# One whole K or V tile in every 50 MB of traffic is sent over four DMA engines

## The chip, the cores and the metric

The kernel runs on one core of one Trainium2 chip. The core has a matrix engine (TensorE, called PE in the profile), a vector engine (DVE), a scalar engine (ACT), a general engine (POOL), a queue engine (SP) that issues most transfers here, and sixteen DMA engines that move the data between the chip's memory (HBM) and the on-chip memory (SBUF, 128 partitions). The metric is the device time of one execution in microseconds (us): the median of several runs. Lower is better.

## The reference

Two layers run twice, in the order A, B, A, B, and the gradient of everything with respect to the input, both caches and all weights is returned with the output. Layer A is one decode step of grouped-query attention over a long cache; layer B is a two-layer MLP on one token for each of two batch rows.

```python
B, Sq, D = 2, 1, 1024
Hq, Hkv, Sk, Dh = 32, 4, 16384, 128        # A: 32 query heads share 4 cached K/V heads, 16384 positions
F = 3584                                    # B: hidden width

def _A_ref(x, k_cache, v_cache, wq, wo):
    q = heads(x @ wq)
    k = jnp.repeat(k_cache, 8, axis=1); v = jnp.repeat(v_cache, 8, axis=1)
    p = _softmax(jnp.einsum("bhqd,bhkd->bhqk", q, k) * (Dh ** -0.5))
    o = jnp.einsum("bhqk,bhkd->bhqd", p, v)
    return merge(o) @ wo
def _B_ref(x, w1, b1, w2, b2):
    return _gelu(_layernorm(x) @ w1 + b1) @ w2 + b2
# x -> x + A(ln x) -> x + B(ln x) -> x + A(ln x) -> x + B(ln x); then jax.vjp with grad_out
```
(`heads` and `merge` stand for reshapes that are cut here.) Everything is bfloat16. K and V are 33.5 MB each, and the gradients of K and V are as large again. Since the work for each cached value is small, the kernel is largely a matter of moving bytes: K and V are read for both forward passes, for the first backward pass and once more for the second one, and the two cache gradients are written.

## The kernel before: how tiles are loaded and stored

The cache is cut into tiles of 1 MB: 128 partitions, each with 32 positions of 128 values, so one run of 8192 bytes for each partition. Seven such buffers (`ld`) are filled in turn by SP; eight more tiles (and two extra) stay resident between the passes.

```python
    LDW = 4096
    NLD = 7
    ld = ctx.enter_context(tc.tile_pool(name="ld", bufs=NLD))
    ... # cut
    def w_load(W, j0, rb, n_cols):
        wt = ld.tile([128, LDW], BF16, name="wt", tag="ld")
        wv = wt[:, 0:rb * n_cols].rearrange("p (j n) -> p j n", j=rb)
        nc.sync.dma_start(wv, W[j0 * 128:(j0 + rb) * 128, :].rearrange("(j p) n -> p j n", p=128))
        return wv
    ... # cut
    Kv = A_k_cache.rearrange("b h (p t) d -> (b h) p t d", p=128)
    Vv = A_v_cache.rearrange("b h (p t) d -> (b h) p t d", p=128)
    ... # cut
    def kv_load(w, g, c):
        keep = w + str(c) if g == G - 1 else w if (g, c) == (XG, 0) else None
        t = held_tiles[keep] if keep else ld.tile([128, LDW], BF16, name="kv_" + w, tag="ld")
        if keep not in held:
            src = Kv if w == "K" else Vv
            nc.sync.dma_start(t[:].rearrange("p (t d) -> p t d", d=128), src[g, :, c * TC:(c + 1) * TC, :])
            if keep:
                held.add(keep)
        return t[:].rearrange("p (t d) -> p t d", d=128)
```

A forward pass (`attn_fwd`) walks over slots of eight 128x128 blocks: TensorE turns a block of K (the name `tp`), DVE or ACT copies it out (`kT`), TensorE makes the scores (`sc`); blocks of V go straight into the weighted sum (`acc_all`). The first backward pass (`attn_bwd`) does the like with both. The second one is the last stage of the kernel. It loads K, V and slices of wq through a list of jobs into whatever tile is free, and it writes the gradients of the caches and the weights:

```python
    def store(out_ap, view, tile_):
        pace["queue"].dma_start(out_ap, view)        # POOL's queue; SP's for the last few
        if tile_ is not None:
            by_store.append(tile_)
    ... # cut
    def load_next():
        job = jobs.popleft()
        t = loaded[job] = load_tile()                # may have to wait for a store to land
        open_loads.append(job)
        if job[0] == "wq":
            src = wq_v[:, job[2]:job[2] + 4, job[1] * D:(job[1] + 1) * D]
            nc.sync.dma_start(t[:].rearrange("p (j n) -> p j n", j=4), src)
        else:
            src = (Kv if job[0] == "K" else Vv)[job[1], :, job[2] * TC:(job[2] + 1) * TC, :]
            nc.sync.dma_start(t[:].rearrange("p (t d) -> p t d", d=128), src)

    def pump(most, spare):
        while jobs and len(open_loads) < most and n_free() > spare:
            load_next()
```

Of the kernel before, what the change touches and what calls it, by code (L numbers as in the profile page):

```python
# [2 lines left out]

# [20 lines left out]
def kernel(  # L24
# [24 lines left out]
    nc = tc.nc  # L49
# [4 lines left out]
    B, _, D = A_x.shape  # L54
# [11 lines left out]
    TC = 32  # L66
# [23 lines left out]
    ps_x = ctx.enter_context(tc.tile_pool(name="ps_x", bufs=4, space=PSUM))  # L90
    ps_acc = ctx.enter_context(tc.tile_pool(name="ps_acc", bufs=1, space=PSUM))
    ps_sm = ctx.enter_context(tc.tile_pool(name="ps_sm", bufs=1, space=PSUM))

    def pt(shape, dtype, name):
        return ps_tp.tile(shape, dtype, name=name, tag="tp")
# [74 lines left out]
    def wide_in(x2):  # L170

        return x2.unsqueeze(1).to_broadcast([128, WIDE // 2, 2])

    def wide_out(ps, c0):

        return ps[:, c0:c0 + WIDE].rearrange("p (a b) -> p a b", b=2)
# [77 lines left out]
    def w_load(W, j0, rb, n_cols):  # L254
        wt = ld.tile([128, LDW], BF16, name="wt", tag="ld")
        wv = wt[:, 0:rb * n_cols].rearrange("p (j n) -> p j n", j=rb)
        nc.sync.dma_start(wv, W[j0 * 128:(j0 + rb) * 128, :].rearrange("(j p) n -> p j n", p=128))
        return wv

    class BwdPipe:  # L260
# [57 lines left out]
    def turn(view, new_tp):  # L318

        tp = new_tp()  # L320
        for o in range(8):
            PE.transpose(tp[:, o, :], view[:, o * 128:(o + 1) * 128], ident[:])  # L322
        evac_bf16(view, tp[:].rearrange("p a b -> p (a b)"), 1024)
# [19 lines left out]
    class Ahead:  # L343
# [9 lines left out]
        def load(self, k):  # L353
            j0, rb = self.chunks[k]
            wv = w_load(self.W, j0, rb, D)
            for j in range(rb):
                self.rows[j0 + j] = wv[:, j, :]
# [46 lines left out]
    def kv_load(w, g, c):  # L404
        keep = w + str(c) if g == G - 1 else w if (g, c) == (XG, 0) else None
        t = held_tiles[keep] if keep else ld.tile([128, LDW], BF16, name="kv_" + w, tag="ld")
        if keep not in held:
            src = Kv if w == "K" else Vv
            nc.sync.dma_start(t[:].rearrange("p (t d) -> p t d", d=128), src[g, :, c * TC:(c + 1) * TC, :])
            if keep:  # L410
                held.add(keep)
        return t[:].rearrange("p (t d) -> p t d", d=128)
# [462 lines left out]
    wq_v = A_wq.rearrange("(j p) n -> p j n", p=128)  # L875

    def wq_steps(l, kv, dqT, dn, new_tp, new_ps, get_=None, done_=lambda *job: None):

        hs = slice(kv * 8, kv * 8 + 8)
        box = {}  # L880

        def load(j):
            wt = ld.tile([128, LDW], BF16, name="wqt", tag="ld") if get_ is None else get_("wq", kv, j)
            box[j] = wt[:].rearrange("p (j n) -> p j n", j=4)
            if get_ is None:
                nc.sync.dma_start(box[j], wq_v[:, j:j + 4, kv * D:(kv + 1) * D])

        def turn_row(j):
            turn(box[j - j % 4][:, j % 4, :], new_tp)

        def products(j0=0):
            ps = new_ps()
            for j in range(j0, DJ):
                for o in range(8):
                    PE.matmul(wide_out(ps, 2 * j), lhsT=box[j - j % 4][:, j % 4, o * 128:(o + 1) * 128],
                              rhs=wide_in(dq_all[:, kv * 8 + o, 2 * l:2 * l + 2]), start=(o == 0), stop=(o == 7))
            V.tensor_tensor(out=dn[:, j0:DJ], in0=dn[:, j0:DJ],
                            in1=ps[:, 2 * j0:2 * DJ].rearrange("p (j b) -> p j b", b=2), op=ALU.add)
            for j in (0, 4):
                done_("wq", kv, j)  # L900

        def dq_in():
            for b in range(2):
                V.tensor_copy(out=dq_all[:, hs, 2 * l + b], in_=dqT[:, b * HKV + kv, :])

        return [lambda j=j: load(j) for j in (0, 4)], dq_in, [lambda j=j: turn_row(j) for j in range(DJ)], products, box
# [31 lines left out]
    for k in range(NLD - 2, len(w2b.chunks)):  # L938
        w2b.load(k)
        j0, rb = w2b.chunks[k]  # L940
# [193 lines left out]
    def load_tile():  # L1134
        return (by_read or by_store if opening["on"] else by_store or by_read).popleft()

    def store(out_ap, view, tile_):
        pace["queue"].dma_start(out_ap, view)
        if tile_ is not None:
            by_store.append(tile_)  # L1140

# [10 lines left out]
    def dbias(rows, i, n, out_ap, name):  # L1152
        p = 32 * i
        row = new_home()
        for c0 in range(0, n, 512):
            ps = mx()
            PE.matmul(ps[p:p + 1, :], lhsT=ones_bf[p:p + 4, 0:1], rhs=rows[p:p + 4, c0:c0 + 512], start=True, stop=True,
                      tile_position=(p, p))
            evac_cast(row[p:p + 1, c0:c0 + 512], ps[p:p + 1, :], 512)
        store(out_ap.rearrange("(o f) -> o f", o=1), row[p:p + 1, 0:n], row)  # L1160

    def dw_units(xrows, yrows, i, chunks, y0, ny, out_of):

        ps_, tpos = (slice(0, 128), None) if i is None else (slice(32 * i, 32 * i + 4), (32 * i, 0))
        box = {}
        units = []
        for j0, rb in chunks:
            for j in range(rb):
                for c0 in range(0, ny, 512):
                    def u(j0=j0, rb=rb, j=j, c0=c0):  # L1170
                        if j == 0 and c0 == 0:
                            box["t"], box["n"] = new_home(), 2 if i is None or pace["short"] else rb
                        sv_ = box["t"][:, 0:rb * ny].rearrange("p (j n) -> p j n", j=rb)
                        ps = mx()
                        PE.matmul(ps[:], lhsT=xrows[ps_, (j0 + j) * 128:(j0 + j + 1) * 128],  # L1175
                                  rhs=yrows[ps_, y0 + c0:y0 + c0 + 512], start=True, stop=True, tile_position=tpos)
                        evac_cast(sv_[:, j, c0:c0 + 512], ps[:], 512)
                        if c0 + 512 >= ny and (j % box["n"] == box["n"] - 1 or j == rb - 1):
                            js = j - j % box["n"]
                            store(out_of(j0 + js, j + 1 - js), sv_[:, js:j + 1], box["t"] if j == rb - 1 else None)  # L1180
                    units.append(Unit(u, j == 0 and c0 == 0))
        return units
# [15 lines left out]
    def load_next():  # L1198
        job = jobs.popleft()
        t = loaded[job] = load_tile()  # L1200
        open_loads.append(job)
        if job[0] == "wq":
            src = wq_v[:, job[2]:job[2] + 4, job[1] * D:(job[1] + 1) * D]
            nc.sync.dma_start(t[:].rearrange("p (j n) -> p j n", j=4), src)
        else:
            src = (Kv if job[0] == "K" else Vv)[job[1], :, job[2] * TC:(job[2] + 1) * TC, :]
            nc.sync.dma_start(t[:].rearrange("p (t d) -> p t d", d=128), src)

    def pump(most, spare):
        while jobs and len(open_loads) < most and n_free() > spare:  # L1210
            load_next()
# [35 lines left out]
    def kv_pair(w, i, h):  # L1247

        g, c = chunks[i]
        if h == 0:  # L1250
            stgs[w, i] = new_home()
        sv_ = stgs[w, i][:].rearrange("p (b r t d) -> p b r t d", r=4, t=2, d=128)
        blk, Qm = blks[w, i], qms[w, g]
        o = 0 if w == "V" else NB
        pss = [mx() for _ in range(4)]
        for b in range(2):
            for r in range(4):
                PE.matmul(pss[r][:, b * 256:(b + 1) * 256], lhsT=blk[32 * r:32 * r + 32, o + 2 * h + b, :],  # L1258
                          rhs=Qm[32 * r:32 * r + 32, :, :].rearrange("p a b -> p (a b)"), start=True, stop=True,
                          tile_position=(32 * r, 0))  # L1260
        for r in range(4):
            evac_cast(sv_[:, 2 * h:2 * h + 2, r], pss[r][:].rearrange("p (b t d) -> p b t d", b=2, t=2), 512)
        if h == 0:
            split[w, i] = pace["short"] or i >= NC - 2
        if h == 1 or split[w, i]:
            lo = h if split[w, i] else 0
            dst = (dVv if w == "V" else dKv)[g, :, c * TC + lo * TC // 2:c * TC + (h + 1) * TC // 2, :]
            store(dst, stgs[w, i][:, lo * LDW // 2:(h + 1) * LDW // 2].rearrange("p (t d) -> p t d", d=128),
                  stgs[w, i] if h == 1 else None)
# [214 lines left out]
    i, g = NC - 1, order[-1]  # L1484
    kv = g % HKV
# [57 lines left out]
```

## Time and profile before

| what | before |
|---|---|
| median of 3 runs | 1142.67 us (1141.52 to 1146.9) |
| span of the profiled run | 1136.9 us |
| TensorE matmul busy | 944.5 us (83%) |
| DVE busy | 633.7 us (56%) |
| ACT busy | 564.7 us (50%) |
| bytes moved by DMA | 449.31 MB, mean 395 GB/s |
| HBM read, written | 348.14 MB, 98.58 MB |

A profile page gives for each engine the busy time, then the span in 40 slices (here 28.4 us each) with the busy tenths of the engines, the share of the sixteen DMA engines that was busy and the rate. The queues of the transfers have numbers: q1 holds what SP issues, q0 what POOL issues, q8 and q14 fetch the engines' own instructions:

```profile
## 3 DMA queue, kind: packets, MB, share of 16 engines
q1 hardware_dynamic: 74448, 354.46, 77.4%
q0 software_dynamic: 17360, 92.29, 19.7%
q8 instruction: 137, 2.24, 0.7%
q14 instruction: 38, 0.31, 0.1%
```

The last column is the time of a queue's packets as a share of what sixteen engines could give in the span. Together these are 97.9%.

The trace also holds, for each transfer, sixteen marks: [...] the transfer counts as landed with the last.

### The profile page before, as it was taken

Reading aid. Unit: us, or ns where it says so; the run is one execution under the profiler, and the core shown is the slowest. Engines: PE = TensorE matmul, PEld = TensorE weight load, DVE = VectorE, ACT = ScalarE, POOL = GpSimd, SP = SyncE. Lnnn points to the kernel's source line nnn. Section 1 sums busy time; section 2 is a strip of 40 time slices with the busy share of each in tenths; the row PEclk is TensorE's granted clock in tenths of the full one; section 3 lists DMA queues with packets and bytes.
Section 4 is the critical chain, followed back from the end, with each engine's and each line's share of the span. In section 5 each row is a group of like instructions: output and inputs, shape, how many; then the busy total and the mean of one; then the engine's idle time right before and its main releaser. Section 6 shows DMA issues by size and latency. Waiting matters only on the chain.

```text
span 1136.9 us, 40053 instructions
## 1 busy us (share of the span) xinstructions
PE 944.5 (83%) x17566; PEld 730.9 (64%) x17567; DVE 633.7 (56%) x1356; ACT 564.7 (50%) x1415; POOL 70.9 (6%) x126
## 2 busy tenths in 40 slices
PE   4989895487879885899988689989898989999884
PEld 3867674487767665888876578855555555555551
DVE  1545451133545432554846454678877868786784
ACT  0535351022535340343554344667777767786673
POOL 0000000000000000000000000022111112111210
PEclk9989796596999876899998799998987868896895
DMA  8999999998999989999999999998999999999996
GB/s 370 424 425 423 425 424 413 409 378 354 424 425 423 425 310 413 408 369 411 367 422 418 351 359 355 346 378 318 376 421 423 421 419 421 421 422 420 423 423 256
DMA packets 91983, 449.31 MB, mean 395 GB/s; under 512 B 7318, under 2 KB 7318, under 8 KB 54688
## 3 DMA queue, kind: packets, MB, share of 16 engines
q1 hardware_dynamic: 74448, 354.46, 77.4%
q0 software_dynamic: 17360, 92.29, 19.7%
q8 instruction: 137, 2.24, 0.7%
q14 instruction: 38, 0.31, 0.1%
HBM read 348.14 MB, written 98.58 MB: 393 GB/s over the span
## 4 chain that ended last, share of the span: by engine, by line
PE 55%; DMA 23%; DVE 11%; ACT 6%; issue 4%; POOL 0%; DVEq 0%; ACTq 0%; POOLq 0%
DMA kv_V<-in_A_v_cache_dram 13%; PE tp L420 10%; PE tpm L1450 5%; PE wtp L270 5%; PE acc_all L452 4%; PE xm L1258 4%; PE xm L1175 3%; DMA wt<-in_A_wo_dram 3%; PE sc L573 3%; DMA kv_K<-in_A_k_cache_dram 3%; PE dp L1312 3%; PE turn L322 3%; DMA keepK<-in_A_v_cache_dram 2%; PE dp L672 2%; DVE big L164 2%
## 5 line engine op out<-in xcount | busy, mean ns | idle before, releaser
L153 ACT COPY kT<-tp 128x512 int32<-128x512 int32 x209 | 122.6, 586 | 253.6 <-PE tp L420 242.5
L156 DVE COPY kT<-tp 128x1024 bf16<-128x1024 bf16 x159 | 108.6, 691 | 110.0 <-PE tp L420 97.8
L420 PE MATMUL tp<-ident,kv_K 128*128 128x128 bf16 x1728 | 145.5, 234 | 4.3 <-DMA kv_K<-in_A_k_cache_dram 4.2
L420 PEld LDWEIGHTS <-kv_K 128*128 128x128 bf16 x1728 | 110.2, 104 | 5.1 <-DMA kv_K<-in_A_k_cache_dram 4.8
L164 DVE CAST big<-xm 128x512 bf16<-128x512 f32 (+1 forms) x125 | 81.2, 686 | 24.6 <-PE xm L1258 16.8
L573 PEld LDWEIGHTS <-kT 128*128 128x128 bf16 x2048 | 76.6, 98 | 28.1 <-issue 21.9
L573 PE MATMUL sc<-qT_bf,kT 128*128 128x8 bf16 x2048 | 92.2, 172 | 0.9 <-issue 0.7
L161 ACT CAST big<-xm 128x512 bf16<-128x512 f32 (+1 forms) x139 | 75.6, 593 | 25.2 <-PE xm L1258 16.2
L420 PE MATMUL tp<-ident,kv_V 128*128 128x128 bf16 x864 | 70.8, 229 | 10.7 <-DMA kv_V<-in_A_v_cache_dram 9.0
L270 PE MATMUL wtp<-ident,wt 128*128 128x128 bf16 x928 | 74.8, 227 | 3.4 <-issue 2.2
L537 ACT ACTIVATE e_all<-sc,negm 128x64 bf16<-128x64 f32 x256 | 77.0, 344 | 1.3 <-DVE negm L532 1.2
L306 PEld LDWEIGHTS <-wt 128*128 128x128 bf16 x1696 | 48.9, 103 | 44.3 <-issue 14.9
L161 ACT CAST keepV<-xm 128x512 bf16<-128x512 f32 x116 | 63.5, 595 | 24.1 <-PE xm L1258 18.4
L452 PE MATMUL acc_all<-kv_V,e_all 128*16 128x256 bf16 x864 | 45.6, 291 | 25.5 <-DVE acc_all L435 12.3
L156 DVE COPY wT<-wtp 128x1024 bf16<-128x1024 bf16 (+1 forms) x64 | 40.7, 641 | 46.6 <-PE wtp L270 43.0
L153 ACT COPY wT<-wtp 128x512 int32<-128x512 int32 (+1 forms) x60 | 34.2, 571 | 62.5 <-PE wtp L270 48.2
L164 DVE CAST keepV<-xm 128x512 bf16<-128x512 f32 x88 | 56.9, 685 | 14.1 <-PE xm L1258 9.5
L164 DVE CAST keepK<-xm 128x512 bf16<-128x512 f32 (+1 forms) x86 | 55.8, 685 | 16.1 <-PE xm L1258 10.8
L420 PEld LDWEIGHTS <-kv_V 128*128 128x128 bf16 x864 | 55.8, 102 | 11.7 <-DMA kv_V<-in_A_v_cache_dram 9.7
L161 ACT CAST keepK<-xm 128x512 bf16<-128x512 f32 (+1 forms) x96 | 52.0, 592 | 16.7 <-PE xm L1258 15.2
L537 ACT ACTIVATION_READ_ACCUMULATOR e_all<-sc,negm 128x1 f32 x256 | 60.2, 236 | 0.0
L270 PEld LDWEIGHTS <-wt 128*128 128x128 bf16 x928 | 57.2, 101 | 4.1 <-issue 2.7
(366 smaller groups left out, 1785.0 us busy)
## 6 DMA issues: line engine op xcount, KB each, us to landing
kv_K<-in_A_k_cache_dram SPq DMA_DIRECT2D x81, 1024.0 KB, 11.8
kv_V<-in_A_v_cache_dram SPq DMA_DIRECT2D x81, 1024.0 KB, 12.2
wt<-in_A_wo_dram SPq DMA_DIRECT2D x32, 1024.0 KB, 10.3
wt<-in_B_w_dram SPq DMA_DIRECT2D x32, 896.0 KB, 14.1
out_dram<-big POOLq DMA_DIRECT2D x25, 1024.0 KB, 16.8
out_dram<-keepK POOLq DMA_DIRECT2D x18, 1024.0 KB, 19.8
wt<-in_A_wq_dram SPq DMA_DIRECT2D x16, 1024.0 KB, 9.0
wt<-in_B_w_dram SPq DMA_DIRECT2D x14, 1024.0 KB, 12.9
```

The source lines that it names most:

```text
L153: S.copy(out=dst.bitcast(I32), in_=src.bitcast(I32))
L156: V.tensor_copy(out=dst, in_=src)
L161: S.copy(out=dst, in_=src)
L164: V.tensor_copy(out=dst, in_=src)
L270: PE.transpose(tp[:, o, :], wv[:, j, (o0 + o) * 128:(o0 + o + 1) * 128], ident[:])
L306: PE.matmul(fps[:, jo, :].rearrange("p (a b) -> p a b", b=2), lhsT=wv[:, j, jo * 128:(jo + 1) * 128], rhs=xT_bf[:, j0 + j, :].unsqueeze(1) ...
L420: PE.transpose(tp[:, j, :], cv[:, b * 8 + j, :], ident[:])
L452: PE.matmul(self.acc[cg:cg + 16, :], lhsT=coef(u), rhs=self.cv[:, t:t + 2, :].rearrange("p t d -> p (t d)"), start=False, stop=True, tile_ ...
L537: S.activation(out=e_all[:, g, f * half:(f + 1) * half, l, h, :], in_=sc[g][f][:, h, :].rearrange("p (a b) -> p a b", b=2), func=ACT.Exp, ...
L573: PE.matmul(sc[g][f][:, :, t % TH], lhsT=kT[:, j, :], rhs=q_bf[:, g, :], start=True, stop=True)
L1258: PE.matmul(pss[r][:, b * 256:(b + 1) * 256], lhsT=blk[32 * r:32 * r + 32, o + 2 * h + b, :], rhs=Qm[32 * r:32 * r + 32, :, :].rearrange(" ...
L1450: PE.transpose(tp[:, j, :], cv[:, b * 8 + j, :], ident[:])
```

## The change

The total of the bytes that have been asked for is counted while the program is built. When it passes 25 MB, and then at every 50 MB, the next K or V tile isn't loaded with one transfer of 128 partitions, but with one of 124 and one of 4. [...] those four move the whole tile (256 KB each, in place of the 64 KB that each of sixteen engines has of an ordinary tile), and the other twelve move nothing of it. It is meant to even out the sixteen engines, if the four have less to do otherwise. Nothing else is changed: the bytes, the tiles and the work of the computing engines stay.

```diff
+    moved = {"mb": 0.0, "next": 25}
+
+    def count_dma(ap):
+        moved["mb"] += math.prod(ap.shape) * 2 / 2.0 ** 20
+
+    def load_plain(dst, src):
+        count_dma(dst)
+        nc.sync.dma_start(dst, src)
+
+    def load_kv(dst, src):
+
+        count_dma(dst)
+        if moved["mb"] < moved["next"]:
+            nc.sync.dma_start(dst, src)
+            return
+        moved["next"] += 50
+        nc.sync.dma_start(dst[0:124], src[0:124])
+        nc.sync.dma_start(dst[124:128], src[124:128])
 ... (w_load and the two loads of wq: nc.sync.dma_start becomes load_plain)
@@ kv_load
-            nc.sync.dma_start(t[:].rearrange("p (t d) -> p t d", d=128), src[g, :, c * TC:(c + 1) * TC, :])
+            load_kv(t[:].rearrange("p (t d) -> p t d", d=128), src[g, :, c * TC:(c + 1) * TC, :])
@@ store
         pace["queue"].dma_start(out_ap, view)
+        count_dma(view)
@@ load_next
-            nc.sync.dma_start(t[:].rearrange("p (t d) -> p t d", d=128), src)
+            load_kv(t[:].rearrange("p (t d) -> p t d", d=128), src)
```

More of the change, by code (lines that the diff above doesn't have):

```diff
@@ L1 @@
+import math
 from collections import deque
@@ L256, in w_load @@
         wv = wt[:, 0:rb * n_cols].rearrange("p (j n) -> p j n", j=rb)
-        nc.sync.dma_start(wv, W[j0 * 128:(j0 + rb) * 128, :].rearrange("(j p) n -> p j n", p=128))
+        load_plain(wv, W[j0 * 128:(j0 + rb) * 128, :].rearrange("(j p) n -> p j n", p=128))
         return wv
@@ L885, in load @@
             if get_ is None:
-                nc.sync.dma_start(box[j], wq_v[:, j:j + 4, kv * D:(kv + 1) * D])
+                load_plain(box[j], wq_v[:, j:j + 4, kv * D:(kv + 1) * D])
         def turn_row(j):
@@ L1203, in load_next @@
             src = wq_v[:, job[2]:job[2] + 4, job[1] * D:(job[1] + 1) * D]
-            nc.sync.dma_start(t[:].rearrange("p (j n) -> p j n", j=4), src)
+            load_plain(t[:].rearrange("p (j n) -> p j n", j=4), src)
         else:
             src = (Kv if job[0] == "K" else Vv)[job[1], :, job[2] * TC:(job[2] + 1) * TC, :]
-            nc.sync.dma_start(t[:].rearrange("p (t d) -> p t d", d=128), src)
+            load_kv(t[:].rearrange("p (t d) -> p t d", d=128), src)
     def pump(most, spare):
```

## The prediction

> **What bounds the kernel now.** I read the slices of the page first, then a table by stage, then the chain of waits at the start of a stage, then what SP's queue waits for, and last the completion marks of single transfers.
>
> The slices (28.4 us each):
>
> ```profile
> PE   4989895487879885899988689989898989999884
> ...
> DMA  8999999998999989999999999998999999999996
> GB/s 370 424 425 423 425 424 413 409 378 354 424 425 423 425 310 413 408 369 411 367 422 418 351 359 355 346 378 318 376 421 423 421 419 421 421 422 420 423 423 256
> ```
>
> See the plateau of 419 to 425 GB/s in slices 1 to 5, 10 to 13 and 29 to 38. In the trace's packet records a full packet of 8192 bytes takes 309 ns at the median, which is 26.5 GB/s, and 16 engines at that rate give 424 GB/s. So on the plateau every one of the sixteen is busy without a break: there is no idle engine that could be filled.
>
> The same by stage (columns: window, its length, busy us and instruction counts of PE, PEld, DVE, ACT and POOL, granted clock, DMA share, GB/s):
>
> ```profile
> 28.00:206.00 178.00, 144.65 (x2863) 119.84 (x2864) 73.29 (x161) 70.86 (x314) 0.00 (x0) 0.83 1.02 422
> 263.00:418.00 155.00, 134.50 (x2804) 112.96 (x2800) 71.56 (x157) 70.13 (x309) 0.00 (x0) 0.89 1.01 416
> ...
> 483.00:560.00 77.00, 74.36 (x1677) 65.06 (x1675) 41.41 (x85) 34.67 (x61) 0.00 (x0) 1.00 0.98 379
> 560.00:635.00 75.00, 62.53 (x1227) 51.11 (x1225) 41.23 (x94) 35.73 (x65) 0.00 (x0) 0.89 1.02 419
> ...
> 730.00:820.00 90.00, 78.53 (x1269) 52.77 (x1267) 69.73 (x138) 64.27 (x126) 18.45 (x33) 0.94 0.94 353
> 820.00:1112.00 292.00, 260.41 (x3449) 159.39 (x3449) 225.05 (x393) 210.41 (x401) 45.67 (x74) 0.81 1.02 421
> ```
>
> Both forward passes (28 to 206, 263 to 418), the second half of the first backward pass (560 to 635) and the last stage (820 to 1112) are bound by the DMA engines. From 483 to 560 TensorE is busy 74.36 of 77 us and sets the pace; around 730 to 820 the rate drops to 353 GB/s.
>
> The chain of waits at the start of the second forward pass, and what SP's queue waits for in the last stage (total us, times, longest us):
>
> ```profile
> 263.50 7.55 DMA kv_K<-in_A_k_cache_dram
> ...
> 293.41 9.72 DMA kv_V<-in_A_v_cache_dram
> ...
> 306.50 15.02 DMA kv_V<-in_A_v_cache_dram
> ...
> 324.14 12.26 DMA kv_V<-in_A_v_cache_dram
> ```
>
> ```profile
> SPq L1207 <- DMA out_dram<-big: 82.0, 12, 20.1
> SPq L1207 <- DMA out_dram<-keepV: 64.5, 12, 12.2
> ```
>
> A pass begins with a wait for its first K tile, and goes on from landing to landing; in the last stage loads wait for stores to land.
>
> Now the engines one by one. Each transfer leaves sixteen completion marks. Time of each before the last one, us, from the trace:
>
> ```
> issued  last     sixteen marks, us before the last
>  19.20   35.16   1.63 1.60 1.59 1.59 1.52 1.49 1.44 1.41 1.38 1.35 1.32 1.28 1.18 0.07 0.01 0
> 139.27  155.75   4.44 4.37 4.34 4.29 4.03 3.58 2.99 2.41 1.70 1.66 1.66 1.44 1.36 0.27 0.03 0
> 389.62  401.71   4.58 4.58 4.57 4.47 4.16 4.07 3.66 3.34 1.68 1.56 1.54 1.51 0.41 0.36 0.13 0
> 942.83  968.79  14.02 13.60 13.59 13.54 9.84 9.80 8.51 8.02 7.99 7.73 6.88 6.57 4.88 4.68 4.68 0
> 1124.40 1133.05  5.96 5.95 5.92 5.90 5.89 5.88 5.88 5.86 5.86 5.85 5.84 5.83 5.83 5.82 5.81 0
> ```
>
> Four marks lie close together at the front (within 0.15 us at 155 and 402). The others fall behind in steps, as they would if the fetches of instructions (queue q8: 137 packets of 16384 bytes, some 0.9 us each) fell to twelve engines only. That the four are engines 0 to 3 is my guess, from what the change is for. The lead grows slowly: from 35 to 155 us the mean lag of the other twelve behind the four goes from 0.5 to 2.6 us. At the end one engine alone is 5.8 us late, and its packets run alone until 1135.2.
>
> [...] The trace of before has 16 marks for every tile, [...] the trace has 26.5 GB/s, and I use that. [...] in the last stage, with two queues full, the spread reaches 14 us where it was under 6 us with one.
>
> **The change part by part.** It removes no byte. The built program shows eight split tiles. By their place in SP's list they stand, in before, at 54.4, 263.5, 311.8, 483.2, 580.7, 726.9, 861.2 and 980.9 us.
>
> Cost of one: an ordinary tile gives each engine 8 packets, 8 x 0.309 = 2.5 us. A split one gives engines 0 to 3 31 + 1 = 32 packets, 9.9 us, and the rest none. So the four get 7.4 us more and the other twelve 2.5 us less: a shift of 9.9 us. Against it stands a mean lag that grows by 2.1 us in 120 us, which is about 50 MB. The dose is over four times what this imbalance asks for, so on the plateau the four become the slowest. What a tile then costs is 7.4 us less the lead that the four had over the slowest.
>
> - 54.4 us, first forward pass: the lead is 4.4 us at 155 and 5.9 us at 216, just past its end. 7.4 less about 5: +2 us.
> - 263.5 and 311.8, the second forward pass, two in one stretch without slack, and the first of them the tile on which the chain waits: 14.8 less 4.6 (the lead at 402): +10 us.
> - 483.2: SP issues it 18 us before TensorE first reads a V tile there (501.2), while V tiles land in 7.2 us at the median. Seven more fit. +0.5 us.
> - 580.7: plateau, lead 2.3 us: +5 us.
> - 726.9: its landing is early enough, slack up to 820 takes most of the imbalance: +1 us.
> - 861.2 and 980.9, last stage. The lone late engine is relieved of 2 x 2.5 = 4.9 us, if it is one of 4 to 15. The four get 14.8 us; they had run out of work at some 1114 to 1116, so they now work until about 1130 and then have the last four stores of 512 KB (1.2 us each) still to do: some 1133 to 1136, where the late engine ended at 1135.2. Net -3 to +2; I take -1, and +0 to +2 for tiles that come late within the stage.
>
> Sum: 2 + 10 + 0.5 + 5 + 1 - 1 + 1 = 18.5 us. No engine's instructions change, and eight more issues of some 0.33 us on SP are hidden.
>
> **The rivals.**
> (a) The dose fits: if the lag in the last stage is what counts (at 968 us the twelve are 7.0 us behind the four in the mean, after some 140 us of plateau), 9.9 us for each 50 MB is nearly right, the lone late engine is relieved, and the kernel gains at the end while the forward passes hide their share. For it: the numbers of 25 and 50 MB look tuned, and the late engine is real. Against: the plateau has no idle engine, so evening out can win only the last 5 to 6 us and one or two at the end of each stage. It would give 1132 to 1142.
> (b) Engines 0 to 3 aren't the leading four. Then nothing is deducted: 7.4 + 14.8 + 1 + 7 + 2 and about 8 in the last stage, +40 us: some 1183.
> (c) It is hidden: seven buffers in flight, 12 us from issue to landing, so one late share of 7 us never reaches TensorE. For it: TensorE is 81 to 87% busy in the forward passes and could catch up. Against: a plateau gives no chance to catch up, as all later tiles queue behind on the same four engines. About 1143 to 1148.
>
> **Range and chances.** I give the sum above about 55%, (a) 20%, (c) 15%, (b) 10%. That pulls the centre a little below 1142.67 + 18.5 = 1161, to 1157 us. Range 1138 to 1171. Faster by over 2% (under 1119.8) isn't to be had from evening out: 0.02. Slower by over 2% (above 1165.5) needs the sum to be a little too small, or (b): 0.27. Within 2%: 0.71.
>
> **What would show it.** In the profile of the changed kernel: slices of the second forward pass below 424 GB/s right after a split tile, as twelve engines wait; marks with four engines last, by some 3 to 10 us, in place of four first; the second forward pass (first K tile to the end of its scores) longer by about 10 us, the stretch 483 to 560 unchanged; the lone engine of the last 5 us gone or replaced by four. The prediction is wrong if the forward passes keep their length (then c), if they get shorter or the last stage does by more than 6 us (a), or if the four were never ahead (b).

## The result, and the profile after

The changed kernel takes 1237.72 us (median of four executions, 1235.38 to 1238.41), the kernel before 1142.1 us (four executions, 1141.36 to 1146.9). The ratio is 1.0824, with a 95% interval of 1.079 to 1.0858: the change costs 95.6 us. The profiled spans are 1136.9 and 1236.6 us.

The marks show what carries a split tile. In the trace of before, a transfer of 128 partitions leaves sixteen marks; the loads of two rows and of one leave three and two. In the changed kernel, a transfer of 124 or of 4 partitions leaves five: one early (see the last section) and four at its end. Those of the first split tile are at 81.39, 82.24, 82.88 and 83.95 us for 124 partitions, and at 82.17, 82.84, 83.49 and 84.38 for 4. Each of these, and each of the sixteen of a tile, is read here as one engine's. That is the author's assumption; the end of before agrees with it. There a store's last mark (1133.05 us) comes 5.8 us after its other fifteen, and from 1130 us on the packets run one at a time, those of 4096 bytes in 159 ns (26 GB/s), where sixteen engines give 424. So four engines carry a split tile, with an estimated 32 packets each (128 rows over four). Which four of the sixteen isn't shown; "0 to 3" in the prediction and the expectations is only a name for them.

Slices of the page of the changed kernel (30.9 us each, counted from 1 here; tenths of busy time for PE and DMA):

```profile
PE   4848895572867896778994779988888789988786
...
DMA  9999999989998998999998999998999999999996
GB/s 374 423 281 401 406 411 412 398 339 238 346 344 306 390 414 326 415 234 352 391 415 224 388 332 369 336 295 345 376 419 419 394 360 420 403 390 344 421 421 261
```

The plateau at 424 GB/s has holes. Slices 3, 10, 18 and 22 move 281, 238, 234 and 224 GB/s, and each lies where a split tile is under way. The row above them is what matters: the DMA digit stays at 8 or 9 in the holes. The engines are not idle there. They are busy and move half as much.

Windows of the changed kernel, one inside each of the eight split tiles, in their order (window, its length, busy us and counts of PE, PEld, DVE, ACT and POOL, granted clock, DMA share, GB/s):

```profile
64.00:84.00 20.00, 2.96 (x60) 2.45 (x57) 2.97 (x6) 4.40 (x28) 0.00 (x0) 0.61 1.02 229
282.00:304.00 22.00, 2.50 (x88) 2.31 (x84) 0.29 (x2) 0.00 (x0) 0.00 (x0) 0.50 1.02 215
360.00:373.00 13.00, 2.36 (x44) 2.10 (x42) 2.85 (x6) 4.69 (x30) 0.00 (x0) 0.71 0.98 212
538.00:558.00 20.00, 12.72 (x279) 12.37 (x276) 6.07 (x9) 5.85 (x10) 0.00 (x0) 0.88 1.00 177
652.00:671.00 19.00, 4.91 (x85) 3.95 (x82) 4.43 (x10) 2.77 (x5) 0.00 (x0) 0.59 1.02 237
811.00:822.00 11.00, 9.92 (x235) 6.87 (x231) 6.12 (x14) 6.03 (x13) 1.64 (x3) 1.00 0.99 222
965.00:970.00 5.00, 4.68 (x63) 2.81 (x62) 4.27 (x7) 3.87 (x9) 1.06 (x2) 0.89 1.02 348
1093.00:1099.00 6.00, 5.69 (x80) 3.39 (x79) 5.52 (x11) 5.42 (x12) 0.75 (x2) 1.00 1.01 296
```

The DMA share is 0.98 to 1.02 in all of them, at 177 to 237 GB/s in the first six, and TensorE does 2.5 us of work in 22 in the second. The same stretch of the list in both kernels, by the DMA view of 66 to 80 us, first before, then after:

```profile
DMA packets 815, 5.94 MB, mean 424 GB/s; under 512 B 91, under 2 KB 91, under 8 KB 91
q1 hardware_dynamic: 814, 5.92, 100.6%
```

```profile
DMA packets 410, 3.08 MB, mean 220 GB/s; under 512 B 35, under 2 KB 35, under 8 KB 35
q1 hardware_dynamic: 409, 3.06, 101.6%
```

Half the packets fill the same time, so a packet takes twice as long. The packet records say so too: the median of a packet of 8192 bytes is 309 ns before and 612 ns after in this window, and 98% of the packets after take over 400 ns. They are not only those of the split tile: at 102% of the time of sixteen engines, the whole tiles on the other twelve are slow as well.

The chain of waits shows what it costs the computing engines (start and length in us; `issue` is time in which the profile names no wait):

```profile
63.17 33.29 DMA kv_V<-in_A_v_cache_dram
...
279.56 27.44 DMA kv_K<-in_A_k_cache_dram
...
359.10 27.81 DMA kv_V<-in_A_v_cache_dram
...
544.94 1.72 issue
...
553.86 4.22 issue
```

Before, the second forward pass began with a wait of 7.55 us for its first K tile. Now that wait is 27.44 us. DMA makes up 36% of the chain after, 23% before.

How late the same VectorE instruction runs, after against before, gives the cost by place:

```
time in before, us    45    207    270    302    419    483    561    641    731    851    978   1060   1117   end
later in after, us  -1.3   16.2   16.2   36.1   49.8   51.4   63.2   79.4   78.5   83.2   92.2   98.3  103.3  99.7
```

It is a staircase with a step at each split tile: 16.2, then 19.9 and 13.7, then 11.8, then 16.2, and some 24 in smaller steps up to 1117. The end gives back 3.6. (These are the two profiled executions, whose spans differ by 99.7 us.)

### The profile page after: what moved, and what is told of

Same layout as the page of the kernel before. It is cut to its first block, busy times and chain, and to the rows that moved or that the text cites. A ratio compares the mean times of both kernels' runs of the same rounds, so it can differ in the third digit from the quotient of the medians.

```text
span 1236.6 us, 40073 instructions
## 1 busy us (share of the span) xinstructions
PE 960.2 (78%) x17567; PEld 741.2 (60%) x17567; DVE 634.1 (51%) x1356; ACT 565.7 (46%) x1415; POOL 70.9 (6%) x126
## 4 chain that ended last, share of the span: by engine, by line
PE 45%; DMA 36%; DVE 9%; ACT 5%; issue 4%; POOL 0%; DVEq 0%; ACTq 0%; SPq 0%; POOLq 0%
DMA kv_V<-in_A_v_cache_dram 16%; PE tp L440 8%; DMA kv_K<-in_A_k_cache_dram 7%; PE wtp L290 5%; PE tpm L1471 4%; PE acc_all L472 3%; DMA wt<-in_A_wo_dram 3%; PE xm L1279 3%; DMA out_dram<-big 3%; DMA out_dram<-keepK 2%; PE turn L342 2%; PE sc L593 2%; PE xm L1196 2%; PE dp L1333 2%; DMA keepK<-in_A_v_cache_dram 2%
## 5 line engine op out<-in xcount | busy, mean ns | idle before, releaser
L290 PE MATMUL wtp<-ident,wt 128*128 128x128 bf16 x928 | 78.1, 234 | 4.0 <-issue 2.8
L326 PEld LDWEIGHTS <-wt 128*128 128x128 bf16 x1696 | 48.8, 103 | 43.1 <-issue 15.3
L176 DVE COPY wT<-wtp 128x1024 bf16<-128x1024 bf16 (+1 forms) x64 | 40.6, 641 | 58.2 <-PE wtp L290 54.5
L173 ACT COPY wT<-wtp 128x512 int32<-128x512 int32 (+1 forms) x60 | 34.2, 571 | 68.5 <-PE wtp L290 60.6
L290 PEld LDWEIGHTS <-wt 128*128 128x128 bf16 x928 | 59.8, 105 | 4.7 <-issue 3.4
```

The lines of the kernel that those rows point to most:

```text
L173: S.copy(out=dst.bitcast(I32), in_=src.bitcast(I32))
L176: V.tensor_copy(out=dst, in_=src)
L290: PE.transpose(tp[:, o, :], wv[:, j, (o0 + o) * 128:(o0 + o + 1) * 128], ident[:])
L326: PE.matmul(fps[:, jo, :].rearrange("p (a b) -> p a b", b=2), lhsT=wv[:, j, jo * 128:(jo + 1) * 128], rhs=xT_bf[:, j0 + j, :].unsqueeze(1) ...
```

## The experiments

All start from the changed kernel. Its core is:

```diff
         moved["next"] += 50
         nc.sync.dma_start(dst[0:124], src[0:124])
         nc.sync.dma_start(dst[124:128], src[124:128])
```

Each time is compared with executions of the kernel before on the same chip. The theories in words: the slow packets come from the four loaded engines; from the source rows; from there being two transfers; or from the partitions that a transfer writes (theory D). Which engine writes which partition isn't shown by any trace, so an engine's "own" partitions are an assumption of theory D. Uneven shares come on top in any case.

**1. Only the first tile is split.**

```diff
-        moved["next"] += 50
+        moved["next"] += 10000
```

> Only the first of the eight split tiles is left (issued at about 53 us). Theory T (while a split tile is on its way, the packets of all sixteen engines take about twice as long, and each split tile pays for itself, 10 to 20 us): the span grows by 14 to 18 us over before, all of it between 60 and 100 us. Rival I (the four engines stay behind and the loss builds up from tile to tile): less than 8 us.

1155.71 against 1141.29 us, ratio 1.0118 (1.0037 to 1.0199): +14.4 us for one tile. By the interval alone it could be 4 to 23 us; in the trace the VectorE instruction at 207 us is 15.3 us late, and the delay stays between some 15 and 21 us to the end. So the first tile costs its time in its own stage, without the other seven, and little of it is paid back. Packets from 66 to 80 us: 614 ns at the median, as in the changed kernel.

**2. Two halves of 64 partitions.** The author took their shares to be even over sixteen engines; that isn't shown.

```diff
-        nc.sync.dma_start(dst[0:124], src[0:124])
-        nc.sync.dma_start(dst[124:128], src[124:128])
+        nc.sync.dma_start(dst[0:64], src[0:64])
+        nc.sync.dma_start(dst[64:128], src[64:128])
```

> The eight tiles are split as 64 and 64 partitions[...]. Theory T (it is the four engines that slow the others) and rival I: within 3 us of before. Rival X (two transfers for one tile, their semaphores and the second issue cost the time): as much as the change, 95 us.

1163.3 us, ratio 1.0184 (1.0086 to 1.0283), +22 us. Neither of the expected costs came, at most 3 us or 95, and packets slow down. The DMA view of 64 to 69 us, in which both halves are under way:

```profile
DMA packets 174, 1.17 MB, mean 234 GB/s; under 512 B 32, under 2 KB 32, under 8 KB 32
q1 hardware_dynamic: 173, 1.16, 99.9%
```

The median packet takes 561 ns, and nearly all are slow from 63 to 70 us, some 7 us for the tile. 7 x (1 - 234/424) = 3.1 us, or an estimated 25 us for eight tiles, where 22 were measured (10 to 32 by the interval). That leaves nothing for uneven shares. So the four loaded engines don't seem to be needed for slow packets.

**3. 112 and 16 partitions.**

```diff
-        nc.sync.dma_start(dst[0:124], src[0:124])
-        nc.sync.dma_start(dst[124:128], src[124:128])
+        nc.sync.dma_start(dst[0:112], src[0:112])
+        nc.sync.dma_start(dst[112:128], src[112:128])
```

> The eight tiles are split as 112 and 16 partitions[...]. Theory D (what slows all is that engines write into partitions that belong to another engine's share): packets of 8192 bytes take clearly more than 309 ns while such a tile moves, 2 to 3 us lost for a tile, 15 to 25 us in all. Theory F (it takes few engines with much work): within 3 us of before.

1157.86 us, ratio 1.0137 (1.0061 to 1.0212), +16.6 us; 546 ns and 246 GB/s from 64 to 69 us, as theory D expected. A number of partitions that sixteen divides does not help.

**4. Another source for the split tiles.** Each is read from one contiguous block of 1 MB, in place of 128 rows that lie apart. The tiles then hold other positions of the cache than the reference asks for.

```diff
-    def load_kv(dst, src):
+    def load_kv(dst, src, row=None):
...
+        if row is not None:
+            src = row
         nc.sync.dma_start(dst[0:124], src[0:124])
...
+    Kr = A_k_cache.rearrange("b h (c p t) d -> (b h c) p t d", p=128, t=TC)
+    Vr = A_v_cache.rearrange("b h (c p t) d -> (b h c) p t d", p=128, t=TC)
... (the two calls of load_kv pass a row of Kr or Vr)
```

> The split as in the change, 124 and 4, but the source is one contiguous block of 1 MB (rows 8 KB apart in HBM, in place of 32 KB), so those eight tiles hold other positions of the cache than the reference's. Theory S (four engines that read rows 32 KB apart collide in HBM): packets are back at 309 ns, and only the uneven shares cost, 20 to 40 us in all. Theory D (the destination): no change, 90 to 100 us over before.

1239.26 us, ratio 1.0849 (1.0763 to 1.0936), and 620 ns a packet: the same as the change. So the distance of the source rows, 32 KB or 8 KB, has no part in it.

**5. Two transfers, split by columns.** Each writes all 128 partitions, half of each row.

```diff
-        nc.sync.dma_start(dst[0:124], src[0:124])
-        nc.sync.dma_start(dst[124:128], src[124:128])
+        nc.sync.dma_start(dst[:, 0:16], src[:, 0:16])
+        nc.sync.dma_start(dst[:, 16:32], src[:, 16:32])
```

> The eight tiles are loaded in two transfers again, but each has all 128 partitions and half of the columns[...]. Theory D (the destination: engines outside their own partitions): within 3 us of before, packets at their ordinary length. Rival X (two transfers for one tile cost 2 to 3 us): some 20 us, as with 64 and 64.

1142.23 against 1142.2 us, ratio 0.9998 (0.9979 to 1.0016). Packets keep 309 ns, those of half the size take 159. That there are two transfers costs nothing that shows.

**6. 127 and 1 partitions, the first tile only.** One engine carries both, as the rate below shows.

```diff
-        moved["next"] += 50
-        nc.sync.dma_start(dst[0:124], src[0:124])
-        nc.sync.dma_start(dst[124:128], src[124:128])
+        moved["next"] += 10000
+        nc.sync.dma_start(dst[0:127], src[0:127])
+        nc.sync.dma_start(dst[127:128], src[127:128])
```

> Only the first of the eight tiles, as 127 and 1 partitions, which one engine carries: 128 packets. Theory D in its narrow form (an engine outside its own partitions shares the way with the one owner at a time): the one engine is at some 600 ns a packet, or 80 us for the tile, the other fifteen stay at 309 ns; 60 to 75 us lost. Theory D in its wide form (one such engine slows all): all packets of the stretch are over 450 ns. Without any slowing: 128 x 0.309 = 40 us for the tile, 33 to 37 us lost.

1180.04 us, ratio 1.0333 (1.0276 to 1.039), +37.8 us. Most of this is something else. The timeline of SP's issues (start and length in us):

```profile
53.64 9.25 SPq L112 DMA_DIRECT2D kv_K<-in_A_k_cache_dram  x1
63.00 16.38 SPq L108 DMA_DIRECT2D kv_V<-in_A_v_cache_dram  x1
```

An issue that takes 0.33 us otherwise takes 9.25 and 16.38 us behind 127 rows for one engine, and the other fifteen run dry: the rate falls to 23 to 29 GB/s, and one packet of 8192 bytes in 309 ns is 26.5. So the time, though near the 33 to 37 us named for the case without any slowing, doesn't decide. From 64 to 80 us that engine works alone, over all partitions, at 309 ns a packet, not 600. Once the others are back (80 to 101 us), 19% of the packets take over 400 ns. Neither form of theory D came as it was put. The DMA share is 0.88 there, so some of the 19% are packets that start on an engine that had run dry; of those that start while all engines are at work, some 10% are slow. So neither writing all over the partitions nor being the only engine slows a packet; it seems to take other engines at work beside it.

**7. 120 and 8 partitions.**

```diff
-        nc.sync.dma_start(dst[0:124], src[0:124])
-        nc.sync.dma_start(dst[124:128], src[124:128])
+        nc.sync.dma_start(dst[0:120], src[0:120])
+        nc.sync.dma_start(dst[120:128], src[120:128])
```

> The eight tiles as 120 and 8 partitions[...]. Theory D: packets at 500 to 650 ns while such a tile moves, 15 to 25 us lost in all, as with 112 and 16. If it takes few engines: within 4 us of before.

1168.06 us, ratio 1.0228 (1.0174 to 1.0282), +25.9 us; 579 ns and 221 GB/s from 64 to 69 us; the cost lies just above the 15 to 25 us of theory D. The packets are nearly as slow as in the change (612 ns). How many engines carry the 120 rows isn't shown.

**8. The uneven share alone.** The tile is loaded whole, and at each of the eight places a transfer of 4 x 24 rows is added, from HBM to HBM. This adds 6.3 MB that nobody reads. Four engines then carry an estimated 32 packets (8 of the tile and 24), as in a split tile, and none of the added ones writes into SBUF. That there are four is taken from experiment 9, where a transfer of four rows leaves four marks; that they are the four of a split tile is the author's assumption.

```diff
-        nc.sync.dma_start(dst[0:124], src[0:124])
-        nc.sync.dma_start(dst[124:128], src[124:128])
+        nc.sync.dma_start(dst, src)
 ... (row counts the places; SPARE and Krows are tensors of 4 x 24 rows for each)
+        nc.sync.dma_start(SPARE[row], Krows[row])
```

> The eight tiles are loaded whole, over sixteen engines, and at each of the eight places one further transfer from HBM to HBM is added (24 rows of 8192 bytes for each of four engines, into a tensor that nothing reads): the uneven shares of the change, without a write into SBUF outside the own partitions. Theory D: the packets beside it stay at 309 ns; what is lost is the uneven share alone, at most 24 x 0.309 = 7.4 us a tile less the lead of the four, 15 to 50 us in all. Theory F (four engines with much work slow all the others): 80 us or more, packets over 500 ns.

1176.4 us, ratio 1.0301 (1.0249 to 1.0353), +34.2 us. The DMA view of 66 to 80 us:

```profile
DMA packets 809, 5.94 MB, mean 424 GB/s; under 512 B 85, under 2 KB 85, under 8 KB 85
q1 hardware_dynamic: 808, 5.92, 100.3%
```

The load is as uneven as in the change, by that reckoning, and the rate is 424 GB/s. So the uneven share doesn't slow a packet; it makes tiles late. By the same VectorE instructions as above:

```
time in before, us    45    207    270    302    419    483    561    641    731    851    978   1060   1117   end
later in this, us   -0.7    4.9    4.0   11.7   16.7   18.4   21.0   25.9   24.8   34.4   35.3   39.5   42.6  38.2
```

(The profiled execution ends 38.2 us later than that of before, the median time is 34.2 longer.) If the two costs simply add, 95.6 - 34.2, an estimated 61 us of the change, come from the slow packets.

**9. Who leads.** Whole tiles; behind one in every 25 MB a tiny transfer of four rows, whose four marks tell how far the engines that carry it have come. That these are the four of a split tile is the author's assumption, not shown. It adds some KB.

```diff
-        moved["next"] += 50
-        nc.sync.dma_start(dst[0:124], src[0:124])
-        nc.sync.dma_start(dst[124:128], src[124:128])
+        moved["next"] += 25
+        nc.sync.dma_start(dst, src)
 ... (row counts the places; SPARE and Krows are tensors of 4 rows of 512 bytes for each)
+        nc.sync.dma_start(SPARE[row], Krows[row])
```

> All tiles whole; after a tile in every 25 MB one tiny transfer (4 rows of 512 bytes, HBM to HBM) follows in the same queue, carried by engines 0 to 3, so that its four marks tell where those engines stand among the sixteen marks of the tile. Time within 6 us of before. If engines 0 to 3 are the four in front (as the prediction guessed), the four marks come together and early, 2 to 4 us before the tile's last mark late in a forward pass. If they are not, they are spread over the sixteen or late.

1142.33 against 1141.32 us, ratio 1.0003 (0.9973 to 1.0032). Marks of the tile, and of the four engines in the tiny transfer behind it, in us before the tile's last:

```
at 129.9  tile  3.30 3.15 3.11 3.08 2.83 2.33 2.28 1.83 1.73 0.42 ... 0
          tiny  2.97 2.64 2.09 1.65
at 389.2  tile  4.44 4.21 4.17 4.16 4.14 3.59 3.29 2.83 1.54 1.52 1.51 1.43 1.34 1.33 0.10 0
          tiny  4.03 3.99 3.11 2.65
```

Put 0.17 us earlier, each of the four falls on a mark of the tile: the second, fifth, seventh and eighth, and the second, fourth, seventh and eighth. So these are four of the first eight engines, but not the first four: neither of the two cases expected. The slowest of the four leads the last engine by 1.8 us and 2.8 us.

**10. 62, 62 and 4 partitions, the first tile only.** The author took it that two engines carry the large parts; that isn't shown.

```diff
-        moved["next"] += 50
-        nc.sync.dma_start(dst[0:124], src[0:124])
+        moved["next"] += 10000
+        nc.sync.dma_start(dst[0:62], src[0:62])
+        nc.sync.dma_start(dst[62:124], src[62:124])
         nc.sync.dma_start(dst[124:128], src[124:128])
```

> Only the first of the eight tiles, as 62, 62 and 4 partitions[...]. If each engine outside its own partitions slows a part of the others, less than all of the packets of the stretch (but more than with one engine) are over 400 ns; if it needs only one or two such engines to slow all sixteen, nearly all of them are. Time lost: 15 to 40 us.

1165.44 us, ratio 1.0206 (1.0154 to 1.0257), +24.1 us. From 66 to 86 us 64% of the packets take over 400 ns (median 502), at a DMA share of 0.96. Beside whole tiles, then, the rate stays at 424 GB/s where whole tiles alone write into SBUF (8), 64% are slow here and 98% in the change; the 19% of experiment 6 hold restarts too. Here too issues took 5.03 and 8.12 us, so the time isn't read as that of slow packets.

**11. Sixteen transfers of 8 partitions, the first tile only.**

```diff
-        moved["next"] += 50
-        nc.sync.dma_start(dst[0:124], src[0:124])
-        nc.sync.dma_start(dst[124:128], src[124:128])
+        moved["next"] += 10000
+        for b in (0, 1, 2, 3, 32, 33, 34, 35, 64, 65, 66, 67, 96, 97, 98, 99):
+            nc.sync.dma_start(dst[b:b + 29:4], src[b:b + 29:4])
```

> The first chosen tile alone is loaded as sixteen transfers of 8 partitions, 4 apart (0, 4, ... 28, then 1, 5, ... 29 and so on; the first eight transfers go to the lower half of the partitions, the last eight to the upper half). [...] the first half runs at 309 ns a packet, some 2.5 us; in the second half the packets of both groups take about 600 ns for some 5 us. Theory 'any tile that isn't loaded as 128 partitions': about 600 ns in both halves, some 10 us. In the time: uneven share of 8 packets (2.5 us) less the lead, and 2.5 us for slowed packets, so +2 to +6 us under the first, +5 to +9 under the second.

1148.04 us in one execution, 1134.55 in the one of before beside it: +13.5, above both ranges (which took it that eight engines carry the tile; that isn't shown). The packets of the first eight transfers took 309 ns, as the first of the two expectations said, where the other had about 600, though they write only the lower half of the partitions and from 64 us on ran beside engines that had run dry. The second eight can't be read: SP spent 17.89 us on the sixteen issues, engines ran dry (120 GB/s from 64 to 69 us, at a DMA share of 0.34), and a packet that finds its engine idle takes longer anyway (316 to 1336 ns for the first ones of the kernel before). For the second half the run decides nothing.

**12. Four transfers of 32 partitions, 4 apart, in all eight tiles.**

```diff
-        nc.sync.dma_start(dst[0:124], src[0:124])
-        nc.sync.dma_start(dst[124:128], src[124:128])
+        for b in range(4):
+            nc.sync.dma_start(dst[b:b + 125:4], src[b:b + 125:4])
```

> Each of the eight chosen tiles is loaded as four transfers of 32 partitions, 4 apart[...]. [...] packets between 309 and 600 ns, mixed, and a cost of at most 1.5 us a tile, 12 us in all. Theory 'any tile that isn't loaded as 128 partitions': 550 to 600 ns throughout and 2.7 us a tile, +20 us or more, as with 64 and 64.

The slices of its page, and its DMA view of 64 to 69 us:

```profile
DMA  9999999988999989999999999997999999999996
GB/s 370 423 425 424 424 425 412 409 351 349 423 425 423 425 303 420 408 353 414 374 421 420 357 356 353 345 353 274 389 397 409 421 422 421 423 422 420 422 423 271
```

```profile
DMA packets 331, 2.13 MB, mean 426 GB/s; under 512 B 72, under 2 KB 72, under 8 KB 72
```

The holes are gone. The median packet of the window takes 309 ns, and over the whole run 2.5% of SP's packets of 8192 bytes take over 400 ns, 2.4% in the kernel before, 12.4% in the change. So a tile need not be loaded as 128 partitions at once. A block of 64, 112, 120 or 124 neighbouring partitions slows the packets (561, 546, 579 and 612 ns), and 32 partitions spread over the tile do not. Of the two expectations, one had packets between 309 and 600 ns, and there were none; the other's 550 to 600 ns didn't come either. The time is 1146.63 us in one execution beside 1134.55 of before, and executions of before range from 1134.55 to 1149.15 in this study, so it isn't told whether the four transfers cost anything.

## Why the prediction was wrong

It gave 1157 us, 1138 to 1171, and a sum of +18.5 us. Measured: +95.6.

- **The step that failed is "Cost of one": "8 x 0.309" and "32 packets, 9.9 us".** It took 309 ns, measured on whole tiles, as a constant of the engine. Between loads a split tile changes it to some 610 ns, for its own packets and for the others while it is under way. 32 x 0.61 = 19.6 us, not 9.9, and the excess over 2.5 is 17.1, not 7.4. Take away a lead of 2 to 3 and 14 to 15 remain: the first tile alone cost 14.4 (experiment 1). In the holes an estimated 54 us are lost: the eight windows above, each length times (1 - GB/s / 424), add up to 9.2 + 10.8 + 6.5 + 11.7 + 8.4 + 5.2 + 0.9 + 1.8 = 54.5. With the 34.2 us of uneven shares (experiment 8) that is 88.7 of 95.6. The windows leave out the edges of the holes; in the fourth and sixth the sum is a little too large, as before had 379 and 353 GB/s there and not 424.
- **The lead was too large.** The prediction deducted about 5 us in the first forward pass and 4.6 in the second. The four of experiment 9 lead the last engine by 1.8 to 2.8 us. If they are the four of a split tile, the guess that those are the front four was half right, rival (b) half true. Experiment 8 keeps 309 ns and so gives the cost of uneven shares by themselves: 4.9 us where 2 was predicted for the first tile, some 12 for the 10 of the second forward pass, 4.9 for the 5 of the tile at 580.7.
- **The slack was too large as well.** In experiment 8 the delay grows by 9.5 us from 731 to 851, where 1 was predicted for the tile at 726.9, and by 8.2 from there to 1117, where the last stage was to be even. That is most of what lies between its 34.2 us and the predicted 18.5.
- **263.5 and 311.8, the second forward pass, were to cost 10 and cost 33.6** (19.9 and 13.7), the largest miss.
- **483.2 us was to cost 0.5 and cost 11.8.** The 18 us of slack were read rightly, but the split tile needs 26 us from issue to its last mark (534.5 to 560.2). Yet it isn't what TensorE is seen to wait for: it landed 1.3 us before TensorE first read a V tile (561.5). TensorE stood still before that, 2.5 us to 546.7 and 4.9 us to 558.1, in which the two `issue` pieces above lie (1.7 and 4.2 us of it); its weights had landed by 537.7. Each time it went on 1.5 us or so after a packet of q8, a fetch of instructions, had landed (545.19 and 556.52); these packets took 1.35 and 1.49 us, where the median before was 0.94. In the kernel before, TensorE's five breaks of over 0.8 us that nothing in the profile ended went on 1.3 to 1.4 us after such a packet too. So late instructions probably cost the time here, and the V tile would hardly have let TensorE start earlier; no run tests it.
- **580.7 was to cost 5 and cost 16.2**, as on the plateau of the first tile. **The last stage** was to be about even; it lost some 20 us from 851 to 1117. There the holes are weaker (348 and 296 GB/s in their windows). 726.9 was to cost 1, and the delay grew by 4.7 from 731 to 851.
- **The relief at the end was right in size, but not by its reason.** One engine alone worked from 1130 to 1135.2 before (26 GB/s), and some 1.5 us at the end after; the end gave back 3.6 us of an expected 4.9. But experiment 8 takes no packet from any engine, and its end gave back 4.3. It may be enough that the late engine catches up while the four are waited for; that split tiles relieve it isn't shown to matter.
- **Some signs were there, but not the sizes.** The second forward pass falls below 424 GB/s at its split tiles. That was to come from twelve engines that wait; it came with all sixteen busy (shares of 1.02 and 0.98), so this sign was met by luck. The stretch from 483 to 560 was to stay unchanged, and grew by 11.8 us. Four marks come last: in the tile that ends at 96.46 us, twelve marks lie at 84.84 to 86.24 and four at 94.74 to 96.46. The gap of 8.5 to 11.6 us reaches just past the 3 to 10 named. Rivals (a) and (c) fell.

What slows the packets? The runs show that it goes with the partitions a transfer writes. Blocks of 64, 112, 120 and 124 have it (561, 546, 579 and 612 ns), partitions spread over the tile don't (309 ns, experiment 12). Experiment 4 rules out the distance of the source rows (620 ns, and 612 in the change), 5 that there are two transfers (309 ns), and 8 the overload (424 GB/s). The trace of the change adds when it happens. In the seventh split tile, from 956 to 966 us, only some 7 packets of loads start per us, near the 6.5 that four engines would give if each had a store between two loads (4 / (0.31 + 0.31), an estimate), and some 54 packets of stores. There the loads take 309 ns at the median and the stores of 4096 bytes 159, as in before. From 966 to 970, when other loads come in, 34% of the loads take over 400 ns. So badly placed writes seem to slow others only where these write into SBUF as well; no run tests this by itself. By which way such writes slow each other isn't shown, as the trace doesn't say which engine wrote which partition. It also stays open why a tile that four engines carry slows the packets of all sixteen (98% over 400 ns from 66 to 80 us).

No version that beats both kernels follows, and none was tried. Only the lone engine's 5 us at the end was to be had, and with the rate kept at 424 GB/s, more load on four engines still cost 34.2 us (experiment 8).

## What to carry to other kernels

Don't take a packet's time for a constant of the engine (309 ns before, 612 in the change): compare the DMA busy share with GB/s, and where the share is full and the rate is half, ask which partitions the transfers write. Load a tile with all 128 partitions, and if it must be split, split it by columns (experiment 5, 309 ns) or, as far as the packets tell, by partitions that are spread over the tile (experiment 12, 309 ns), not by blocks (546 to 612 ns). Before load is moved between engines, a tiny transfer behind a whole one shows how far the engines that carry it are ahead (1.8 and 2.8 us of the last one in experiment 9).

## What the runs showed of the hardware that was not expected

- A badly placed transfer slows its neighbours: from 66 to 80 us in the changed kernel 98% of all packets, those of whole tiles on the other twelve engines with them, took over 400 ns, 612 at the median in place of 309.
- SP's issue, 0.33 us otherwise, can stall: 9.25 and 16.38 us behind 127 rows on one engine, 5.03 and 8.12 us behind the two transfers of 62 rows. Sixteen transfers of 8 rows took 17.89 us to issue. The other engines starve meanwhile, at 23 to 29 GB/s in experiment 6 and 120 in 11.
- Stores are slowed too where many loads are: from 819 to 829 us in the changed kernel stores of 4096 bytes take 328 ns at the median, in place of 159. Beside the seventh split tile, from 956 to 966 us, they keep 159.
- A transfer of 124 or 4 partitions leaves one mark some 0.5 us after its issue (once 1.4) and four more at its end, where a whole tile leaves sixteen.
- TensorE can stand still for its own instructions: the breaks under 483.2 us above ended 1.3 to 1.6 us after a packet of 16384 bytes of q8 had landed, in both kernels. That the fetch is the cause is inferred from these times.
